# A pre-norm block on one core: statistics of one tile moved to ScalarE, the keys' sum moved to VectorE, one tile transposed by DMA

## The chip, the cores and the metric

The kernel runs on one core of one Trainium2 chip. The core has five engines that work side by side, each through its own instructions in order: TensorE (PE; its weight loads are shown as PEld), VectorE (DVE), ScalarE (ACT), GpSimd (POOL) and SyncE (SP), which here issues all transfers. They wait for each other through semaphores. The metric is the device time of one execution, in microseconds. Before the change it was 172.0 us, the median of three runs (171.96 to 172.21).

## The reference

The input x has 2048 rows of 512 columns, in bfloat16. Two sub-blocks follow one another, each with a layer norm in front and a residual around it:

```python
h  = x + attn(layernorm(x), wqkv, wo)      # 32 heads of 16 columns, linear attention
h2 = h + relu(layernorm(h) @ w1) @ w2      # 512 -> 1792 -> 512
```

The attention is linear: with phi(t) = (t + 1 if t > 0 else exp(t)) + 1e-6 it computes

```python
kv  = sum over rows of phi(k) (outer) v    # per head, 16 x 16
z   = sum over rows of phi(k)              # per head, 16
out = phi(q) @ kv / (phi(q) . z + 1e-6)
```

so no 2048 x 2048 matrix appears, but every key must be known before the first row of the attention's output is.

## The kernel before, in words

The 2048 rows are 16 tiles of 128 rows (an index t below), and four chunks of 512 rows, each of four tiles. Everything stays in the core's memory: x, the normalized rows, their transposes `lnT` (one per chunk), phi(k) of every tile (`pk`, kept in `pk_lo` and in the buffer that later holds the MLP's activations), phi(q) transposed (`pqT`), and all weights.

The stages, which overlap, are these.

- **First norm.** VectorE takes mean and variance of a tile (S, A: lines 237 and 238), ScalarE makes 1/sqrt of the variance from Ln and Exp (R: 243, 244), VectorE normalizes (N: 251).
- **Transposes.** Tiles 0 to 5 are transposed on TensorE (T: 270) and copied out by ScalarE (E: 280) or VectorE (V: 283); tiles 6 to 15 are transposed by DMA from SP (X: 291).
- **Keys.** Four matmuls per tile (K: 299), then phi: Exp and Relu on ScalarE (F, U: 317, 320), minimum and sum on VectorE (M, D: 324, 327).
- **G and z.** Values are never formed: G accumulates normalized-x-transposed times phi(k) over the 16 tiles in four PSUM banks (351), and kv follows from G and the value weights (381). The sum z is made on TensorE: for each of four column blocks, 16 matmuls, one per tile, with a right-hand side of ones and one output column (359).
- **Queries.** Per chunk, four groups of four matmuls (Q: 307) and the same phi (qF, qU, qM, qD).
- **Attention output.** kv is masked to heads (kx: 389) and multiplied by wo (m, copied out by mD: 399). The denominator of a chunk is a matmul of phi(q) with the masked z (d4: 406), its reciprocal Ln and Exp on ScalarE (dl4, dx4: 412, 417). In chunk 0 it is spread to all rows of a head by matmuls (rp: 422) and multiplied in on VectorE (rm: 428); in chunks 1 to 3 it is written to DRAM (wb: 434), read back broadcast in eight transfers (rb: 437, tile `rr`) and multiplied in (dm: 444). Four matmuls per tile then give the attention's output (h: 453), and VectorE adds x (hD: 459).
- **Second norm and MLP.** Statistics and mean removal on VectorE (s, a, n: 239, 240, 258), transposes by TensorE for chunk 0 (t, copied out by e: 286 or v: 289) and by DMA for the others (x: 292). The first product has 14 feature groups per chunk (p, and ph in halves for the first four of chunk 0: 468, 477), with ReLU on ScalarE or VectorE (pA: 483, pD: 488). The second has 14 matmuls per tile (f: 497). VectorE scales and adds (fo: 505), and SP writes the tile out (fd: 512).

The text called "block 1" in the change's short name is the norm and MLP part; its first chunk is the one that TensorE transposed.

The order is written out by hand as one list of words, `ORDER`. `T.3.3` means tile 3 through bank 3; `p.0.6.0` means chunk 0, feature group 6, bank 0; `lx.4.2` loads two tiles of x from tile 4 on. Each engine executes its own words in the order of the list, so a word that waits holds back all later words of its engine. Words of different engines do not hold each other except through data and buffers. SP's queue is one such list too, and the semaphores of its transfers are eight, used in turn: a transfer also waits for the one eight before it to land.

Of the kernel before, what the change touches and what calls it, by code (L numbers as in the profile page):

```python
# [58 lines left out]
def kernel(  # L59
# [27 lines left out]
    NO = 4  # L87

    const = ctx.enter_context(tc.tile_pool(name="const", bufs=1))
    big = ctx.enter_context(tc.tile_pool(name="big", bufs=1))  # L90
# [14 lines left out]
    wqkv_v = A_wqkv.rearrange("(k p) n -> p k n", p=P)  # L105
# [27 lines left out]
    z_sb = big.tile([P, KD], F32, name="z_sb")  # L133
    acts = [big.tile([P, KF, CW], BF16, name=f"at{i}") for i in range(2)]
    pk_lo = big.tile([P, 2, D], BF16, name="pk_lo")
    st = big.tile([P, NT, nc.vector.BN_STATS_DIM], F32, name="st")
# [7 lines left out]
    ld = big.tile([P, 2, CW], F32, name="ld")  # L144
    rd = big.tile([P, 2, CW], BF16, name="rd")
# [8 lines left out]
    def pk(t, n=1):  # L154
        return pk_lo[:, t : t + n, :] if t < 2 else acts[0][:, t - 2 : t - 2 + n, :]
# [38 lines left out]
    def op_mask():  # L194
# [4 lines left out]
    def op_maskh():  # L199
# [9 lines left out]
    def op_masks():  # L209
        op_mask()  # L210
        op_maskh()


    def op_gate():
        nc.gpsimd.memset(wk_sb[:, 0:4:2, 0:1], 0.0)

# [4 lines left out]
    def load_d(dst, src, k, n, queue=None):  # L221
        (queue or nc.sync).dma_start(out=dst[:, k : k + n, :], in_=src[:, k : k + n, :])

    op_lk = lambda k, n: load_d(wk_sb, wqkv_v[:, :, D : 2 * D], k, n)
    op_lkA = lambda k, n: load_d(wk_sb, wqkv_v[:, :, D : 2 * D], k, n, nc.scalar)
# [11 lines left out]
    op_S = lambda t: nc.vector.bn_stats(out=st[:, t, :], in_=x_nat[:, t, :])  # L237
    op_A = lambda t: nc.vector.bn_aggr(out=mv[:, t, :], in_=st[:, t, :])
# [116 lines left out]

    def op_z(jb, b):
        at_bank["z"] = b
        for t in range(NT):
            nc.tensor.matmul(  # L359
                bk[:, b, jb : jb + 1], lhsT=pk(t)[:, 0, jb * P : (jb + 1) * P], rhs=ones[:],  # L360
                start=(t == 0), stop=(t == NT - 1),
            )
# [40 lines left out]
    def op_d4(c, b):  # L403
        at_bank["d4", c] = b
        for jb in range(KD):
            nc.tensor.matmul(  # L406
                bk[jb * Q4 : (jb + 1) * Q4, b, :], lhsT=zhd[:, jb, :], rhs=pqT[c][:, jb, :],
                start=True, stop=True,
            )

    def op_dl4(c):
        nc.scalar.activation(
            out=ld[:, c % 2, :], in_=bk[:, at_bank["d4", c], :], func=ACT.Ln, bias=eps6[:], scale=1.0
        )

    def op_dx4(c):
        nc.scalar.activation(out=rd[:, c % 2, :], in_=ld[:, c % 2, :], func=ACT.Exp, scale=-1.0)

    def op_rp(c, jb, b):
        at_bank["rp", c, jb] = b  # L420
        rows = slice(jb * Q4, (jb + 1) * Q4)
        nc.tensor.matmul(
            bk[:, b, :], lhsT=erep[rows, :], rhs=rd[rows, c % 2, :], start=True, stop=True
        )
# [8 lines left out]
    def op_wb(c):  # L433
        nc.sync.dma_start(out=scr[c].rearrange("j h o n -> (j h) (o n)"), in_=rd[:, c % 2, :])
# [113 lines left out]
```

## Time and profile before

| | |
|---|---|
| median of three runs | 172.0 us |
| the profiled execution | 172.15 us |
| its span in the profile | 170.4 us |
| TensorE busy | 165.1 us (97%) |
| VectorE busy | 94.5 us (55%) |
| ScalarE busy | 66.3 us (39%) |
| transfers moved | 14.97 MB |

The span is shorter than the execution by 1.75 us, which lies around it. TensorE's busy time is modelled and matmuls overlap, so its share alone does not say how near it is to its limit; the chain that ended last does, since it goes back from the last instruction, step by step, to what released it. The groups of instructions give a line's total, the mean of one, and how long its engine sat idle just ahead of it.

### The profile page before, as it was taken

Reading aid. Unit: us, or ns where it says so; the run is one execution under the profiler, and the core shown is the slowest. Engines: PE = TensorE matmul, PEld = TensorE weight load, DVE = VectorE, ACT = ScalarE, POOL = GpSimd, SP = SyncE. Lnnn points to the kernel's source line nnn. Section 1 sums busy time; section 2 is a strip of 40 time slices with the busy share of each in tenths; the row PEclk is TensorE's granted clock in tenths of the full one; section 3 lists DMA queues with packets and bytes.
Section 4 is the critical chain, followed back from the end, with each engine's and each line's share of the span. In section 5 each row is a group of like instructions: output and inputs, shape, how many; then the busy total and the mean of one; then the engine's idle time right before and its main releaser. Section 6 shows DMA issues by size and latency. Waiting matters only on the chain.

```text
span 170.4 us, 2460 instructions
## 1 busy us (share of the span) xinstructions
PE 165.1 (97%) x949; PEld 81.4 (48%) x966; DVE 94.5 (55%) x199; ACT 66.3 (39%) x98; POOL 4.7 (3%) x21
## 2 busy tenths in 40 slices
PE   7999999999999999999999999999999999999993
PEld 7554344456444584444444444444444444444463
DVE  3999983215889945399050579105349613450252
ACT  3699754846796853403307213302133000310300
POOL 7300000000000000000000000000000000000000
PEclk9999999999999999999999999999999999999999
DMA  4963955999000022001433000544000240030004
GB/s 128 312 241 71 187 110 127 304 386 295 4 6 0 0 89 69 0 0 22 105 99 82 4 2 13 108 135 150 31 31 0 54 100 0 0 127 0 0 0 123
DMA packets 22619, 14.97 MB, mean 88 GB/s; under 512 B 13264, under 2 KB 21584, under 8 KB 22608
## 3 DMA queue, kind: packets, MB, share of 16 engines
q1 hardware_dynamic: 22608, 14.82, 31.1%
q8 instruction: 7, 0.11, 0.3%
q14 instruction: 4, 0.03, 0.1%
HBM read 9.44 MB, written 2.49 MB: 70 GB/s over the span
## 4 chain that ended last, share of the span: by engine, by line
PE 87%; ACT 4%; DMA 3%; DVE 2%; SPq 2%; issue 1%
PE bk L497 28%; PE bk L468 26%; PE bk L307 8%; PE bk L453 8%; PE bk L299 5%; PE bk L351 5%; DMA wk_sb<-in_A_wqkv_dram 3%; PE bk L477 2%; ACT eb L317 2%; ACT rb L320 1%; SPq L219 1%; PE bk L359 1%; PE bk L406 1%; PE bk L393 1%; PE bk L270 1%
## 5 line engine op out<-in xcount | busy, mean ns | idle before, releaser
L497 PE MATMUL bk<-w_sb,at 128*128 128x512 bf16 (+2 forms) x247 | 49.8, 355 | 0.3
L468 PE MATMUL bk<-lnT,w_sb 128*128 128x512 bf16 x204 | 46.8, 379 | 0.2
L483 ACT ACTIVATE at<-bk 128x1024 bf16<-128x1024 f32 x19 | 19.2, 1023 | 65.7 <-PE bk L468 62.9
L497 PEld LDWEIGHTS <-at 128*128 128x128 bf16 x252 | 23.4, 98 | 25.2 <-issue 0.5
L468 PEld LDWEIGHTS <-w_sb 128*128 128x128 bf16 x208 | 20.4, 98 | 24.3
L488 DVE TENSOR_SCALAR at<-bk 128x1024 bf16<-128x1024 f32 x9 | 11.0, 1225 | 24.7 <-PE bk L468 23.3
L505 DVE SCALAR_TENSOR_TENSOR gT<-bk,rstd,h_nat 128x512 bf16<-128x512 f32 (+2 forms) x18 | 12.2, 689 | 20.0 <-PE bk L497 16.3
L320 ACT ACTIVATE rb<-bk 128x1024 bf16<-128x1024 f32 (+1 forms) x18 | 16.7, 927 | 7.1 <-PE bk L307 5.6
L317 ACT ACTIVATE eb<-bk 128x1024 bf16<-128x1024 f32 (+1 forms) x18 | 16.6, 928 | 4.2 <-PE bk L299 3.5
L299 PE MATMUL bk<-wk_sb,lnT 128*128 128x512 bf16 x63 | 15.2, 379 | 0.6 <-ACT rb L320 0.3
L307 PE MATMUL bk<-lnT,wq_sb 128*128 128x512 bf16 x62 | 15.2, 379 | 0.1
L453 PE MATMUL bk<-m_sb,pqs 128*128 128x512 bf16 x63 | 15.1, 379 | 0.0
L459 DVE TENSOR_TENSOR h_nat<-bk,x_nat 128x512 bf16<-128x512 f32 x16 | 10.8, 687 | 6.8 <-PE bk L453 6.6
L351 PE MATMUL bk<-at,h_nat 128*128 128x512 bf16 x54 | 13.4, 379 | 0.1
L237 DVE BATCH_NORM_STATS2 st<-x_nat 128x6 f32<-128x512 bf16 x16 | 10.3, 677 | 1.8 <-DMA x_nat<-in_A_x_dram 1.8
L239 DVE BATCH_NORM_STATS2 st<-h_nat 128x6 f32<-128x512 bf16 x16 | 10.7, 682 | 0.1
L324 DVE TENSOR_SCALAR eb<-eb 128x1024 bf16<-128x1024 bf16 (+1 forms) x18 | 7.0, 389 | 5.9 <-ACT eb L317 5.9
L299 PEld LDWEIGHTS <-lnT 128*128 128x128 bf16 x64 | 6.1, 98 | 8.2 <-DMA lnT<-h_nat 0.8
L453 PEld LDWEIGHTS <-pqs 128*128 128x128 bf16 x64 | 6.3, 98 | 7.5
L351 PEld LDWEIGHTS <-h_nat 128*128 128x128 bf16 x64 | 6.1, 98 | 6.8
L307 PEld LDWEIGHTS <-wq_sb 128*128 128x128 bf16 x64 | 5.9, 98 | 6.4 <-issue 0.2
L444 DVE TENSOR_TENSOR pqs<-pqT,rr 128x1024 bf16<-128x1024 bf16 x6 | 4.0, 688 | 5.5 <-DMA rr<-scr 5.2
(61 smaller groups left out, 94.4 us busy)
## 6 DMA issues: line engine op xcount, KB each, us to landing
w_sb<-in_B_w_dram SPq DMA_DIRECT2D x4, 896.0 KB, 8.6
out_dram<-gT SPq DMA_DIRECT2D x15, 128.0 KB, 2.0
rr<-scr SPq DMA_DIRECT2D x24, 64.0 KB, 2.6
x_nat<-in_A_x_dram SPq DMA_DIRECT2D x2, 512.0 KB, 6.4
x_nat<-in_A_x_dram SPq DMA_DIRECT2D x4, 128.0 KB, 2.2
wk_sb<-in_A_wqkv_dram SPq DMA_DIRECT2D x2, 256.0 KB, 3.7
x_nat<-in_A_x_dram SPq DMA_DIRECT2D x2, 256.0 KB, 4.1
wq_sb<-in_A_wqkv_dram SPq DMA_DIRECT2D x2, 256.0 KB, 6.1
```

Source lines behind the costliest of these rows:

```text
L299: nc.tensor.matmul(bk[:, b, :], lhsT=lnT[c][:, kd, j * P : (j + 1) * P], rhs=wk_sb[:, kd, :], start=(kd == 0), stop=(kd == KD - 1),)
L307: nc.tensor.matmul(bk[:, b, :], lhsT=wq_sb[:, kd, j * P : (j + 1) * P], rhs=lnT[c][:, kd, :], start=(kd == 0), stop=(kd == KD - 1),)
L317: nc.scalar.activation(out=buf(eb, kind, i, n), in_=bank(at_bank[kind, i], n), func=ACT.Exp)
L320: nc.scalar.activation(out=buf(rb, kind, i, n), in_=bank(at_bank[kind, i], n), func=ACT.Relu)
L351: nc.tensor.matmul(bk[:, KD + kd, :], lhsT=ln_nat[:, t, kd * P : (kd + 1) * P], rhs=pk(t)[:, 0, :], start=(t == 0), stop=(t == NT - 1),)
L453: nc.tensor.matmul(bk[:, b, :], lhsT=pqs[:, (c * KD + jb) % NQ, j * P : (j + 1) * P], rhs=m_sb[:, jb, :], start=(jb == 0), stop=(jb == KD ...
L459: nc.vector.tensor_tensor(out=h_nat[:, t : t + n, :], in0=bank(at_bank["h", t], n), in1=x_nat[:, t : t + n, :], op=ALU.add,)
L468: nc.tensor.matmul(bk[:, b, :], lhsT=w1_sb[:, kd, f * P : (f + 1) * P], rhs=lnT[c][:, kd, :], start=(kd == 0), stop=(kd == KD - 1),)
L483: nc.scalar.activation(out=acts[c % 2][:, f : f + n, :], in_=bank(at_bank["p", c, f], n), func=ACT.Relu)
L488: nc.vector.tensor_scalar(out=acts[c % 2][:, f : f + n, :], in0=bank(at_bank["p", c, f], n), scalar1=0.0, scalar2=None, op0=ALU.max,)
L497: nc.tensor.matmul(bk[:, b, 0 : w * P], lhsT=acts[c % 2][:, f, j * P : (j + 1) * P], rhs=w2_sb[:, f, k * P : (k + w) * P], start=(f == 0), ...
L505: nc.vector.scalar_tensor_tensor(out=o_t[:, t % NO, cols], in0=bk[:, at_bank["f", t, k], 0 : w * P], scalar=rstd2[:, t : t + 1], in1=h_nat ...
```

## The change

Three things are changed in the code, and with them the whole order.

- **Tile 1's statistics** come from ScalarE: a copy that adds up the row (Sa), the negated mean (Sm), a square of the difference that adds up (Sq), and Ln and Exp (Sr). VectorE normalizes from them (Sn, in place of N.1).
- **z.** VectorE adds phi(k) of tiles 2 to 13, two tiles at a time, into fp32 (za, five additions of 1024 columns), adds the two halves (zf), and splits the sum into a bfloat16 part and a bfloat16 rest (zhi, zlo). z on TensorE then has six matmuls per column block instead of 16: the two parts and tiles 0, 1, 14 and 15.
- **Tile 0 of the second norm** is transposed by DMA (x.0) instead of on TensorE (t.0, e.0).

The denominators of all four chunks get buffers of their own (`ld`, `rd`), and those of chunks 2 and 3 are made together (`d4.2.0.2`).

In the new order, among much else: all four warm-up words of 512 columns stand ahead of the transposes; T.2 stands behind K.0; tile 3's copy is V instead of E; x tiles 4 and 5 are loaded ahead of wk; X.8 and X.9 stand ahead of all loads of wq and wv; keys of tiles 12 and 13 come before those of 10 and 11; gD stands behind zc; mD.0 and mD.2 have qM.1.2 between them; the first half of w2 (`l2.0.7`) is loaded behind wb.1 instead of among the other weights; wb.2 stands ahead of the transposes x.4 to x.7.

```diff
 ORDER = """
...
+table const masks warm.70.7.64 lx.0.1 S.0 A.0 warm.3.7 warm.1.7 lx.1.1 lx.2.1 S.2 Sa.1 lx.3.1 lx.4.2 lk.0.2
+lk.2.2 R.0.1 Sm.1 N.0.0.2 S.3 A.2 N.0.2.2 A.3 S.5 Sq.1 Sr.1 Sn.1 T.0.0.0.2 T.0.3.2.2 T.1.1 R.2.2 E.0.2.2
+E.0.0.2 E.1 N.3 T.3.3 S.4 A.5 A.4 R.4.2 lx.6.2 K.0.0 F.0.1 U.0.1 N.2 V.3 N.4 T.2.2 V.2 M.0.1 N.5 D.0.1 K.1.1
...
+A.13 M.4.2 S.12 D.4.2 A.12 R.12.2 X.7 X.6 G.3 K.7.3 K.6.2 X.8 X.9 F.6.2 U.6.2 S.11 S.10 A.10 N.12 M.6.2 A.11
+N.13 R.10.2 G.4 K.8.0 K.9.1 F.8.2 U.8.2 lq.0.2 X.12 X.13 D.6.2 N.11 S.14 S.15 M.8.2 A.14 N.10 A.15 D.8.2
+R.14.2 N.15 za.4 N.14 X.11 X.10 lv.0.2 lq.2.2 X.15 X.14 lv.2.2 l2.7.7 lo.0.2 lo.2.2 l1.2.2 l1.0.2 G.5 G.6 G.7
+K.12.0 K.13.1 G.8 K.11.3 K.10.2 F.12.2 U.12.2 F.10.2 U.10.2 G.9 Q.0.0.0 Q.0.1.1 za.6 za.8 M.10.2 D.10.2 za.10
+M.12.2 D.12.2 K.14.2 K.15.3 G.10 qU.0.0.2 F.14.2 qF.0.0.2 U.14.2 G.11 G.12 G.13 Q.0.2.0 Q.0.3.1 za.12 M.14.2
+qM.0.0.2 zf zhi D.14.2 G.14 zlo z.0.2 G.15 z.2.2 qF.0.2.2 qD.0.0.2 z.1.2 z.3.2 gA.2.2 qM.0.2.2 zc Q.1.1.3
+Q.1.0.2 gD.0.2 qU.0.2.2 qF.1.0.2 qU.1.0.2 zh qD.0.2.2 kv.0.4 kv.3.4 kv.2.4 kv.1.4 qM.1.0.2 kx qD.1.0.2 Q.1.2.0
+Q.1.3.1 qF.1.2.2 m.1.5 m.0.4 m.3.7 d4.0.3 m.2.6 mD.0.2 qM.1.2.2 mD.2.2 Q.2.0.2 dl4.0 dx4.0 qU.1.2.2 Q.2.1.3
+rp.0.0.4 rp.0.1.5 rp.0.2.6 rp.0.3.7 Q.2.3.1 Q.2.2.0 rm.0.0.2 rm.0.2.2 h.0.4 qD.1.2.2 hD.0 h.1.5 h.2.6 qU.2.0.2
+qU.2.2.2 qF.2.2.2 h.3.7 d4.1.4 qF.2.0.2 dl4.1 dx4.1 Q.3.2.0 Q.3.3.1 qF.3.2.2 qU.3.2.2 s.0 hD.1 hD.2 a.0 s.1
+n.0 a.1 hD.3 n.1 s.2 s.3 a.2 Q.3.0.2 t.1.5 Q.3.1.3 a.3 n.2 n.3 v.1 t.2.6 t.3.7 v.2 v.3 x.0 ph.0.2.0.0
...
+pA.0.0.2 p.0.6.0 p.0.7.1 p.0.5.3 p.0.4.2 wb.1 l2.0.7 rb.1.0 rb.1.6 rb.1.2 rb.1.4 rb.1.7 rb.1.5 rb.1.3 rb.1.1
...
+    zacc = big.tile([P, 2, D], F32, name="zacc")
+    zhl = big.tile([P, 2, D], BF16, name="zhl")
...
+    def op_Sa(t):
+        nc.scalar.activation(out=junk[:], in_=x_nat[:, t, :], func=ACT.Copy, accum_out=sums[:, 0:1])
+
+    def op_Sm(t):
+        nc.scalar.activation(out=sums[:, 1:2], in_=sums[:, 0:1], func=ACT.Copy, scale=-1.0 / D)
+
+    def op_Sq(t):
+        nc.scalar.activation(
+            out=junk[:], in_=x_nat[:, t, :], func=ACT.Square, bias=sums[:, 1:2], scale=1.0,
+            accum_out=sums[:, 2:3],
+        )
+
+    def op_Sr(t):
+        nc.scalar.activation(out=sums[:, 3:4], in_=sums[:, 2:3], func=ACT.Ln, bias=eps5[:], scale=1.0 / D)
+        nc.scalar.activation(out=sums[:, 3:4], in_=sums[:, 3:4], func=ACT.Exp, scale=-0.5)
...
+    def op_za(t):
+        nc.vector.tensor_tensor(out=zacc[:], in0=pk(2, 2) if t == 4 else zacc[:], in1=pk(t, 2), op=ALU.add)
+
+    def op_zf():
+        nc.vector.tensor_tensor(out=zacc[:, 0, :], in0=zacc[:, 0, :], in1=zacc[:, 1, :], op=ALU.add)
+
+    def op_zhi():
+        nc.vector.tensor_copy(out=zhl[:, 0, :], in_=zacc[:, 0, :])
+
+    def op_zlo():
+        nc.vector.tensor_tensor(out=zhl[:, 1, :], in0=zacc[:, 0, :], in1=zhl[:, 0, :], op=ALU.subtract)
+
     def op_z(jb, b):
         at_bank["z"] = b
-        for t in range(NT):
-            nc.tensor.matmul(
-                bk[:, b, jb : jb + 1], lhsT=pk(t)[:, 0, jb * P : (jb + 1) * P], rhs=ones[:],
-                start=(t == 0), stop=(t == NT - 1),
+        parts = [zhl[:, i, :] for i in range(2)] + [pk(t)[:, 0, :] for t in range(NT) if not 2 <= t < ZT + 2]
+        for i, part in enumerate(parts):
+            nc.tensor.matmul(
+                bk[:, b, jb : jb + 1], lhsT=part[:, jb * P : (jb + 1) * P], rhs=ones[:],
+                start=(i == 0), stop=(i == len(parts) - 1),
             )
```

More of the change, by code (lines that the diff above doesn't have):

```diff
@@ L207, in op_maskh, with load_d @@
             keep(rows, rows, [[-1, P]], DH - 1, DH)
[L209 to L215, printed above, removed]
     def op_lx(t, n):
         nc.sync.dma_start(out=x_nat[:, t : t + n, :], in_=rows_of(xf, t, n))
-    def load_d(dst, src, k, n, queue=None):
-        (queue or nc.sync).dma_start(out=dst[:, k : k + n, :], in_=src[:, k : k + n, :])
+    def load_d(dst, src, k, n):
+        nc.sync.dma_start(out=dst[:, k : k + n, :], in_=src[:, k : k + n, :])
     op_lk = lambda k, n: load_d(wk_sb, wqkv_v[:, :, D : 2 * D], k, n)
-    op_lkA = lambda k, n: load_d(wk_sb, wqkv_v[:, :, D : 2 * D], k, n, nc.scalar)
     op_lq = lambda k, n: load_d(wq_sb, wqkv_v[:, :, 0:D], k, n)
@@ L237, with op_Sn @@
     op_S = lambda t: nc.vector.bn_stats(out=st[:, t, :], in_=x_nat[:, t, :])
+    def op_Sa(t):
[10 more added lines that the diff above has]
+        nc.scalar.activation(out=sums[:, 3:4], in_=sums[:, 3:4], func=ACT.Exp, scale=-0.5)
+    def op_Sn(t, k=0, n=KD):
+        cols = slice(k * P, (k + n) * P)
+        nc.vector.tensor_scalar(
+            out=ln_nat[:, t, cols], in0=x_nat[:, t, cols], scalar1=sums[:, 1:2], scalar2=sums[:, 3:4],
+            op0=ALU.add, op1=ALU.mult,
+        )
     op_A = lambda t: nc.vector.bn_aggr(out=mv[:, t, :], in_=st[:, t, :])
@@ L399, in op_mD, with op_d4 @@
         nc.vector.tensor_copy(out=m_sb[:, jb : jb + n, :], in_=bank(at_bank["m", jb], n))
-    def op_d4(c, b):
-        at_bank["d4", c] = b
-        for jb in range(KD):
-            nc.tensor.matmul(
-                bk[jb * Q4 : (jb + 1) * Q4, b, :], lhsT=zhd[:, jb, :], rhs=pqT[c][:, jb, :],
-                start=True, stop=True,
-            )
+    def op_d4(c0, b0, n=1):
+        for c, b in zip(range(c0, c0 + n), range(b0, b0 + n)):
+            at_bank["d4", c] = b
+            for jb in range(KD):
+                nc.tensor.matmul(
+                    bk[jb * Q4 : (jb + 1) * Q4, b, :], lhsT=zhd[:, jb, :], rhs=pqT[c][:, jb, :],
+                    start=True, stop=True,
+                )
     def op_dl4(c):
         nc.scalar.activation(
-            out=ld[:, c % 2, :], in_=bk[:, at_bank["d4", c], :], func=ACT.Ln, bias=eps6[:], scale=1.0
+            out=ld[:, c, :], in_=bk[:, at_bank["d4", c], :], func=ACT.Ln, bias=eps6[:], scale=1.0
         )
     def op_dx4(c):
-        nc.scalar.activation(out=rd[:, c % 2, :], in_=ld[:, c % 2, :], func=ACT.Exp, scale=-1.0)
+        nc.scalar.activation(out=rd[:, c, :], in_=ld[:, c, :], func=ACT.Exp, scale=-1.0)
     def op_rp(c, jb, b):
@@ L422, in op_rp @@
         nc.tensor.matmul(
-            bk[:, b, :], lhsT=erep[rows, :], rhs=rd[rows, c % 2, :], start=True, stop=True
+            bk[:, b, :], lhsT=erep[rows, :], rhs=rd[rows, c, :], start=True, stop=True
         )
@@ L433, in op_wb @@
     def op_wb(c):
-        nc.sync.dma_start(out=scr[c].rearrange("j h o n -> (j h) (o n)"), in_=rd[:, c % 2, :])
+        nc.sync.dma_start(out=scr[c].rearrange("j h o n -> (j h) (o n)"), in_=rd[:, c, :])
     def op_rb(c, h):
```

67 lines of the change are left out of this document (27 added, 40 removed).

## The prediction

> **What bounds the kernel now.** I read the page first: how busy each engine is and whose work the final chain is.
>
> ```profile
> PE 165.1 (97%) x949; PEld 81.4 (48%) x966; DVE 94.5 (55%) x199; ACT 66.3 (39%) x98; POOL 4.7 (3%) x21
> ...
> PE 87%; ACT 4%; DMA 3%; DVE 2%; SPq 2%; issue 1%
> ```
>
> TensorE holds 87% of the chain. Its busy figure alone proves little, because matmuls overlap, so I take what one matmul costs from the chain in order of time (start, length, what). Between the edges quoted here it runs through TensorE with no other engine in it.
>
> ```profile
> 3.65 4.60 DMA wk_sb<-in_A_wqkv_dram
> ...
> 8.28 2.33 PE bk L299 x10
> ...
> 36.52 0.38 PE bk L359 x16
> ...
> 48.18 0.33 PE bk L422 x4
> 48.51 2.72 PE bk L307 x12
> 51.23 1.73 PE bk L453 x8
> ...
> 56.41 0.22 PE bk L270 x4
> ...
> 59.52 3.59 PE bk L477 x32
> ...
> 167.68 0.35 DVE gT L505
> ```
>
> A 512-wide matmul costs 1.73/8 = 0.216 us, a transpose 0.22/4 = 0.055, a one-column z matmul (L359) 0.38/16 = 0.024. So every removed TensorE instruction is worth its own time, and every wait inserted from 8.3 us on costs its own length. Stages from the query stage on show how little there is left to win (window, its length, busy of PE, PEld, DVE, ACT, POOL, then clock, DMA share, GB/s):
>
> ```profile
> 43.14:59.45 16.31, 16.20 (x103) 7.60 (x104) 14.85 (x29) 13.04 (x16) 0.00 (x0) 1.00 0.01 2
> 59.45:103.00 43.55, 43.34 (x218) 21.16 (x220) 23.35 (x42) 13.94 (x18) 0.00 (x0) 1.00 0.17 46
> 103.00:167.70 64.70, 64.33 (x324) 30.53 (x327) 27.65 (x50) 11.09 (x15) 0.00 (x0) 1.00 0.20 55
> ```
>
> TensorE idles 0.1, 0.2 and 0.4 us in these stages at full clock; VectorE is full in the first and half free in the MLP. Counting 0.216 per matmul (208 of the first MLP product, 48 of the h product, 210 of the second) gives the same.
>
> **The change, part by part.** Durations (busy, mean ns in the group; then idle before it) that the parts below use:
>
> ```profile
> L459 DVE TENSOR_TENSOR h_nat<-bk,x_nat 128x512 bf16<-128x512 f32 x16 | 10.8, 687 | 6.8 <-PE bk L453 6.6
> ...
> L327 DVE TENSOR_TENSOR pqT<-rb,eb 128x1024 bf16<-128x1024 bf16 x8 | 5.2, 680 | 0.0
> L258 DVE TENSOR_SCALAR hn<-h_nat,mv 128x512 bf16<-128x512 bf16 x16 | 5.0, 342 | 0.1
> ...
> L243 ACT ACTIVATE rstd<-mv,eps 128x2 f32<-128x2 f32 (+2 forms) x13 | 3.8, 292 | 4.0 <-DVE mv L238 3.9
> ...
> L417 ACT ACTIVATE rd<-ld 128x512 bf16<-128x512 f32 x4 | 2.5, 630 | 0.1
> L399 DVE CAST m_sb<-bk 128x1024 bf16<-128x1024 f32 x2 | 2.4, 1220 | 0.4 <-PE bk L393 0.4
> ```
>
> *Keys' sum.* z shrinks from 4x16 to 4x6 matmuls: 40 x 0.024 = **-0.96 us** on the path. [...]
>
> In exchange VectorE gets five fp32 additions of 1024 columns and three operations of 512. No fp32 addition out of SBUF is in the trace. Ends: 680 ns (1024 bf16 columns) and 1220 ns (1024 fp32 columns out of PSUM); I take 1220, since fp32 operands are what the two share: 5 x 1.22 + 3 x 0.61 = 7.9 us. [...]
>
> ```profile
> 33.64 1.29 DVE L327 TENSOR_TENSOR at<-rb,eb 128x1024 bf16<-128x1024 bf16 x2
> 40.38 1.23 DVE L376 CAST gT<-bk 128x1024 bf16<-128x1024 f32 x1 [5.45 <-PE bk L307]
> ```
>
> What hides them is VectorE's idle time in the G and z stage, 5.45 us in this one piece. What can still bind is the end of the series. In the new order the first query exp ends near 35.1 us by my walk; then zf, zhi, D.14, zlo at 0.61 to 0.68 each end D.14 near 37.3 and zlo near 37.9. TensorE reaches G.14 at 38.2 and z.0 at 39.1: spare 0.9 and 1.1. Cost 0; without the cover each late us costs one us.
>
> *Statistics of tile 1 on ScalarE.* VectorE loses S.1 and A.1. ScalarE gains Sa and Sq (128x512, 0.63 each by L417), Sm and the two parts of Sr (0.2 to 0.3 each): about 2 us, into the time before 6 us, where ScalarE idled for VectorE (3.9 us in the L243 row, most of it there). The first loads of x, 128 and 256 KB, landed after this long:
>
> ```profile
> x_nat<-in_A_x_dram SPq DMA_DIRECT2D x4, 128.0 KB, 2.2
> ```
> ```profile
> x_nat<-in_A_x_dram SPq DMA_DIRECT2D x1, 256.0 KB, 3.4
> ```
>
> R.0 now stands behind Sa: x tile 1, second on the queue (issued at 1.26), lands near 3.45 and Sa ends near 4.1, so the first normalized half is ready near 4.9. Warm-up matmuls, all now ahead of the transposes, run to 6.25 anyway. Behind S.5, which waits for x tiles 4 and 5 (issued 0.5 earlier than before, at 2.66, and landing by 6.1), VectorE does tile 1 near 6.6 and tile 3 near 7; K.0 is ready near 7.6 and still waits for wk at 8.25, since the same bytes stand ahead of it on SP's queue. Cost 0, with 0.6 spare. But T.2 moves behind K.0, out of that wait: +0.22. The copy of tile 3 goes from ScalarE to VectorE; both are ahead of K.3 by my walk, so 0.
>
> *Key stage.* The weight loads and matmuls of K.8 waited here:
>
> ```profile
> 18.66 1.89 PE L351 MATMUL bk<-at,h_nat 128*128 128x512 bf16 x8
> 20.81 1.90 PE L299 MATMUL bk<-wk_sb,lnT 128*128 128x512 bf16 x8 [0.26 <-ACT rb L320]
> ```
> ```profile
> 20.80 1.41 PEld L299 LDWEIGHTS <-lnT 128*128 128x128 bf16 x8 [0.75 <-DMA lnT<-h_nat]
> ```
> ```profile
> wq_sb<-in_A_wqkv_dram SPq DMA_DIRECT2D x1, 256.0 KB, 4.3
> lnT<-h_nat SPq DMA_TRANSPOSE x1, 4.2
> ```
>
> The eight matmuls from 18.66 are through at 20.39, so 0.42 is lost; X.8 took 4.2 us to land beside the wv and wq loads. The new SP order puts X.8 and X.9 ahead of lq and lv; at the 2.5 us of the median transpose (quoted below) they land near 18.4 and 19.6 for K.8 at 19.8: **-0.42**. The loads move: lv.0 and lq.2 now stand behind X.10, which waits for N.10 near 23.9. lq.2 is issued at about 25.7 and, at the 4.3 us of its like beside wv and two transposes, lands at 30.0; Q.0.0 needs it at 29.7: **+0.3** (between 0 and 0.4). X.14 (up to 4.2) lands with K.14's turn: 0.
>
> *Queries of chunk 0, block 1.* This chain of VectorE is tight:
>
> ```profile
> 45.62 2.36 DVE L399 CAST m_sb<-bk 128x1024 bf16<-128x1024 f32 x2 [0.36 <-PE bk L393]
> 48.41 0.43 DVE L324 TENSOR_SCALAR eb<-eb 128x1024 bf16<-128x1024 bf16 x1 [0.43 <-ACT eb L317]
> 48.75 2.35 DVE L428 TENSOR_TENSOR pqs<-bk,pqT 128x1024 bf16<-128x1024 f32 x2
> ```
>
> Before, rp started at 48.18, just as the second m copy ended (47.98), and h at 51.23 as rm ended (51.10). After, qM.1.2 (0.34) stands between the two copies, and two Q groups instead of three between rp and h. From the first m matmul, VectorE needs 0.64 + 4x1.135 + 0.34 + 0.1 = 5.6 us to the second rm; TensorE reaches h.0's third matmul after m 0.65, d4 0.33, m 0.22, four Q groups 3.45, rp 0.33, two matmuls 0.43 = 5.4. **+0.25**, against 0.2 lost there before: +0.05.
>
> *DMA transpose of tile 0.* x.0 takes t.0 off TensorE: **-0.22**, and its copy off ScalarE. It is issued when n.0 is through, and takes this long to land (SP's transposes of this kind and of the first kind):
>
> ```profile
> lnT<-hn SPq DMA_TRANSPOSE x12, 2.4
> lnT<-h_nat SPq DMA_TRANSPOSE x10, 2.5
> ```
>
> n.0 ends near 54.7 on VectorE; x.0 lands near 57.2, and the first MLP matmul comes near 58.0: 0.8 spare. From h (51.23) to the MLP (59.52) the chain took 8.3 us and its work 8.1 (32 matmuls 6.9, one d4 group 0.33, 16 transposes 0.88); with t.1 between the Q groups I find no wait, so a further **-0.2**.
>
> *Queue of SP behind it.* l2.0.7 (896 KB of w2) moves from 30 us to behind wb.1, ahead of the eight rr loads; the last of these shares l2's semaphore, so it waits for l2 to land. Loads of that size:
>
> ```profile
> w_sb<-in_B_w_dram SPq DMA_DIRECT2D x2, 896.0 KB, 6.1
> ```
> ```profile
> w_sb<-in_B_w_dram SPq DMA_DIRECT2D x1, 896.0 KB, 12.1
> ```
> ```profile
> rr<-scr SPq DMA_DIRECT2D x24, 64.0 KB, 2.6
> ```
>
> Issued near 56.5, alone, I take 6.1: landed 62.6, last rr at 65.2. dm.1.2, qM, qD and dm.1.0 (2.3 us) then end at 67.5, and h.4 is due at 69.4. Cost 0.
>
> *MLP.* The same work in another order. Walking banks and tiles I find everything in time, by 0.15 to 0.4 us at its tightest (fo.6 before h.14, the ReLU of features 4 and 5 before feature 9, the ReLU of 12 and 13 of chunk 1). Before lost about 0.3 net; I give the same.
>
> *Sum*: -0.96 + 0.22 - 0.42 + 0.3 + 0.05 - 0.22 - 0.2 = -1.2 us. The profiled execution took 172.15 (span 170.4 and 1.75 around it), 0.15 above the median of 172.0; so 170.95 for it and **170.8 us** for the median.
>
> **The rivals.**
>
> *All tight places hold*: lq.2 lands in time, no rm wait, and the MLP's 0.3 goes: 170.8 - 0.3 - 0.25 - 0.3 = 169.95. For it: VectorE is half idle. Against: each of these needs a spare that I could not find.
>
> *VectorE takes the gain back.* z ends the wait of zc and, behind it, of gD, which kv needs. After z, TensorE has two Q groups, 1.73 us; zc and gD need 0.2 + 0.1 + 1.23 = 1.5: 0.2 spare. In the old order gD stood ahead of z. If latencies add 0.5 here, 0.4 more at rm and 0.3 at one of the MLP's tight places, the time is 172.0. For it: three waits with the same engine; against: 14.9 of 16.3 us VectorE was already busy in the stage from 43 us on and still kept up.
>
> *w2 late, slower.* If l2.0.7 takes the 12.1 us of the last load, issued behind others, it lands at 68.6, the last rr at 71.2, dm.1.0 ends at 73.5 and h.4 waits 4.1: 174.9. It begins to cost at 8.0 us of landing and turns the forecast into a loss above 9.2. For it: the rr packets share the same engines. Against: nothing else large is in flight.
>
> **How the numbers follow.** Forecast 52% (own range 170.2 to 171.6), all tight places hold 14%, VectorE takes it back 20% (171.5 to 172.6), slower by w2 or by another transfer that lands late 14%. Taking 0.2%, 0.34 us, as what a measurement can tell: faster 0.52 + 0.14 + 0.07, same 0.06, slower 0.07 + 0.14. The range 169.8 to 172.8 leaves out most of the last case.
>
> **What would show it.** L392 with 24 matmuls in 0.6 us of the chain; no wait of the K loads on a DMA near 20 us; fp32 additions of about 1.2 us, D.14 before TensorE's turn; a wait of some 0.3 us on wq near 30 and of 0.25 on VectorE before rp or h; the MLP beginning near 58.1 instead of 59.5 and ending near 166.4. Wrong if K.0 starts late, if kv or h waits over 0.5 us, or if rr holds h.4.

## The result and the profile after

The changed kernel took 170.88 us, the median of four runs (170.47 to 170.94), against 172.11 (171.96 to 172.24) for the kernel before on the same chip: a ratio of 0.9924 with a 95% interval of 0.9906 to 0.9943. The profiled execution took 170.94 us at a span of 169.2, against 172.15 and 170.4. The page's busy times and the shares of the chain:

```profile
PE 163.5 (97%) x906; PEld 79.9 (47%) x922; DVE 105.1 (62%) x209; ACT 64.2 (38%) x98; POOL 4.8 (3%) x21
...
PE 94%; DMA 2%; issue 1%; SPq 1%; DVE 0%; DVEq 0%
```

TensorE has 43 matmul records fewer and now 94% of the chain instead of 87%; VectorE is 10.6 us busier, and the chain does not go through it for that. To place the difference I cut both spans where TensorE had done the same work: start of K.0, start of K.4, the point where ten key tiles and six G groups are done, start of kv, start of the MLP, and the end of the last matmul. The windows of after, in the columns of the prediction:

```profile
7.93:13.81 5.88, 5.83 (x39) 2.90 (x37) 5.88 (x20) 5.32 (x13) 0.00 (x0) 1.00 0.47 177
13.81:22.44 8.63, 8.63 (x40) 3.88 (x40) 8.44 (x25) 7.03 (x14) 0.00 (x0) 1.00 0.55 107
22.44:42.04 19.60, 19.44 (x111) 9.22 (x113) 16.57 (x30) 12.50 (x15) 0.00 (x0) 1.00 0.79 242
42.04:58.21 16.17, 16.12 (x100) 7.49 (x100) 14.65 (x28) 12.43 (x15) 0.00 (x0) 1.00 0.09 19
58.21:166.53 108.32, 107.78 (x541) 51.49 (x548) 54.36 (x93) 21.94 (x30) 0.00 (x0) 1.00 0.22 59
```

and of before (its stage from kv to the MLP, 16.31 us, stands in the prediction):

```profile
7.51:13.48 5.97, 5.73 (x35) 2.79 (x34) 5.89 (x18) 5.36 (x14) 0.00 (x0) 1.00 0.61 226
13.48:22.55 9.07, 8.81 (x41) 3.84 (x41) 8.81 (x27) 6.65 (x14) 0.00 (x0) 1.00 0.75 135
22.55:43.14 20.59, 20.43 (x150) 10.21 (x152) 8.73 (x20) 12.83 (x15) 0.00 (x0) 1.00 0.80 247
...
59.45:167.66 108.21, 107.67 (x540) 51.69 (x547) 50.98 (x90) 25.03 (x33) 0.00 (x0) 1.00 0.19 52
```

| stretch | before, us | after, us | difference | forecast |
|---|---|---|---|---|
| to the start of K.4 | 13.48 | 13.81 | +0.33 | +0.22 |
| ten key tiles and six G groups | 9.07 | 8.63 | -0.44 | -0.42 |
| from there to kv (holds z and lq.2) | 20.59 | 19.60 | -0.99 | -0.66 |
| kv to the MLP | 16.31 | 16.17 | -0.14 | -0.37 |
| MLP | 108.21 | 108.32 | +0.11 | 0 |
| sum | | | -1.13 | -1.23 |

Every stretch has the sign that was forecast or lies within 0.11 us of zero. The sum is right partly because three errors (+0.11, +0.23, +0.11) and one of -0.33 cancel. The reader is to look at VectorE in the third stretch: 16.57 us busy against 8.73, in a stretch that got 0.99 us shorter.

**z.** In the chain of after, a one-column group of six took 0.13 and the three other groups 0.43:

```profile
39.01 0.13 PE bk L392 x6
39.14 0.89 PE bk L369 x4
40.02 0.43 PE bk L392 x18
```

That is 0.56 us, where before had 0.38 (shown in the prediction) and these two:

```profile
38.65 0.38 PE bk L359 x16
...
40.78 0.78 PE bk L359 x32
```

1.54 - 0.56 = 0.98 us, at 0.43/18 = 0.024 per matmul as before.

**The head.** The path to the first key starts at a load now. From the chain, then from TensorE's timeline (start, length, what, and in brackets the idle time ahead of it with what ended it):

```profile
2.66 3.62 DMA x_nat<-in_A_x_dram
```
```profile
7.37 0.72 PE L288 MATMUL bk<-ident,h_nat 128*128 128x128 bf16 x8 [0.99 <-DVE h_nat L251]
7.93 1.03 PE L317 MATMUL bk<-wk_sb,lnT 128*128 128x512 bf16 x4
8.81 0.40 PE L288 MATMUL bk<-ident,h_nat 128*128 128x128 bf16 x4
9.05 1.89 PE L317 MATMUL bk<-wk_sb,lnT 128*128 128x512 bf16 x8
```

x tiles 4 and 5 landed at 6.28, S.5 could start only then, Sn.1 stood behind it, and T.1 waited for Sn.1. K.0 began at 7.93 and had wk. T.2 (8.81 to 9.05) then stands in the row of keys, 0.24.

**K.8.** No matmul waits; one weight load does, for X.9, inside the shadow of the matmul ahead of it (TensorE, then its weight loads):

```profile
19.85 1.89 PE L317 MATMUL bk<-wk_sb,lnT 128*128 128x512 bf16 x8
```
```profile
20.66 0.59 PEld L317 LDWEIGHTS <-lnT 128*128 128x128 bf16 x4 [0.28 <-DMA lnT<-h_nat]
```

**rp and rm.** Two waits stand here (TensorE, VectorE, weight loads):

```profile
47.78 0.64 PE L456 MATMUL bk<-rd,erep 32*128 32x512 bf16 x4
```
```profile
48.21 2.36 DVE L462 TENSOR_TENSOR pqs<-bk,pqT 128x1024 bf16<-128x1024 f32 x2 [0.23 <-PE bk L456]
```
```profile
50.62 2.70 PEld L487 LDWEIGHTS <-pqs 128*128 128x128 bf16 x14 [0.43 <-DVE pqs L462]
```

The four rp matmuls take from 47.78 to the next query group at 48.35, 0.57 instead of 0.33, because the last two of them go into the banks that mD.2 copies out until 47.98. VectorE is free at 47.98 but starts rm at 48.21, when rp's result is there. Then h.0's third matmul waits for the second rm: h's 16 matmuls take 50.09 to 53.75, 3.66, where 16 x 0.216 is 3.45. Together 0.24 + 0.21 = 0.45 us.

**MLP.** It begins at 58.21. One wait is inside it, at h.11 of chunk 2 (weight loads, then VectorE):

```profile
89.26 0.11 PEld L487 LDWEIGHTS <-pqs 128*128 128x128 bf16 x2 [0.47 <-DVE pqs L478]
89.86 0.11 PEld L487 LDWEIGHTS <-pqs 128*128 128x128 bf16 x2 [0.49 <-DVE pqs L478]
```
```profile
88.51 1.29 DVE L478 TENSOR_TENSOR pqs<-pqT,rr 128x1024 bf16<-128x1024 bf16 x2 [3.97 <-DMA rr<-scr]
```

VectorE idled 3.97 us for the last broadcast loads of chunk 2's denominators, which stand behind the transposes x.5 to x.4 and the write wb.3 on SP's queue. h.11's four matmuls took 89.26 to 90.31, 1.05 instead of 0.86, and began 0.14 late: 0.33 us.

### The profile page after: what moved, and what is told of

Its sections match the earlier page's. It is cut to its first block, busy times and chain, and to the rows that moved or that the text cites. A ratio compares the mean times of both kernels' runs of the same rounds, so it can differ in the third digit from the quotient of the medians.

```text
span 169.2 us, 2382 instructions
## 1 busy us (share of the span) xinstructions
PE 163.5 (97%) x906; PEld 79.9 (47%) x922; DVE 105.1 (62%) x209; ACT 64.2 (38%) x98; POOL 4.8 (3%) x21
## 3 DMA queue, kind: packets, MB, share of 16 engines
HBM read 9.44 MB, written 2.49 MB: 70 GB/s over the span
## 4 chain that ended last, share of the span: by engine, by line
PE 94%; DMA 2%; issue 1%; SPq 1%; DVE 0%; DVEq 0%
PE bk L531 28%; PE bk L502 26%; PE bk L487 9%; PE bk L325 8%; PE bk L317 8%; PE bk L369 8%; DMA x_nat<-in_A_x_dram 2%; PE bk L511 2%; PE bk L288 1%; SPq L214 1%; PE bk L440 1%; PE bk L426 1%; PE bk L414 1%; PE bk L456 0%; PE bk L392 0%
## 5 line engine op out<-in xcount | busy, mean ns | idle before, releaser
L517 ACT ACTIVATE at<-bk 128x1024 bf16<-128x1024 f32 x16 | 16.3, 1024 | 68.1 <-PE bk L502 63.0
L522 DVE TENSOR_SCALAR at<-bk 128x1024 bf16<-128x1024 f32 x12 | 14.7, 1222 | 16.3 <-PE bk L502 15.0
L493 DVE TENSOR_TENSOR h_nat<-bk,x_nat 128x512 bf16<-128x512 f32 x16 | 10.6, 681 | 7.1 <-PE bk L487 6.0
L261 ACT ACTIVATE rstd<-mv,eps 128x2 f32<-128x2 f32 (+2 forms) x12 | 3.5, 294 | 9.2 <-DVE mv L258 7.7
```

The lines of the kernel that those rows point to most:

```text
L493: nc.vector.tensor_tensor(out=h_nat[:, t : t + n, :], in0=bank(at_bank["h", t], n), in1=x_nat[:, t : t + n, :], op=ALU.add,)
L517: nc.scalar.activation(out=acts[c % 2][:, f : f + n, :], in_=bank(at_bank["p", c, f], n), func=ACT.Relu)
L522: nc.vector.tensor_scalar(out=acts[c % 2][:, f : f + n, :], in0=bank(at_bank["p", c, f], n), scalar1=0.0, scalar2=None, op0=ALU.max,)
```

## The experiments

All were measured beside the kernel before on their chip, in three groups. Its median was 172.00 beside E1 to E4, 172.10 beside E5 to E8 and 172.38 beside E9 to E12. The changed kernel itself ran again in the third group (E9). Runs of one kernel lie up to 2.0 us apart (the kernel before beside E5 to E8, 171.55 to 173.54; E2 1.5), which is why medians of 5 to 12 runs are told, and why differences of a few tenths are read from the traces too.

### E1 and E2: z back on TensorE, without and with the additions

E1 takes the eight words of the sum on VectorE out and lets TensorE sum all 16 tiles; E2 does only the second, so that VectorE makes the sums and nobody uses them. In the cut below the eight words, which stand at six places of the order, are put on one line.

```diff
-za.4 za.6 za.8 za.10 za.12 zf zhi zlo
-        parts = [zhl[:, i, :] for i in range(2)] + [pk(t)[:, 0, :] for t in range(NT) if not 2 <= t < ZT + 2]
+        parts = [pk(t)[:, 0, :] for t in range(NT)]
```

> The changed kernel with z as before: 4x16 one-column matmuls on TensorE, and VectorE's additions, their sum and its two halves taken out of the order. Theory (z stood on TensorE's path at 0.024 us a matmul): 40 x 0.024 = 0.96 us slower than the changed kernel's 170.9, so 171.9 (171.6 to 172.1). Rival (z was hidden, since kv waits for the copies of G anyway): 170.9 to 171.2.

> As the run before it, with VectorE's additions left in; their result is not used. Theory (the additions lie in VectorE's idle time): the same time as without them, within 0.2 us. Rival (the additions hold the minimum and sum of the last keys back, and so G): 0.3 us or more slower than without them.

Measured: E1 171.91 (ratio to before 0.9994, 0.9979 to 1.0009), E2 171.83 (0.9990, 0.9976 to 1.0004). Both are 1.0 us above the changed kernel's 170.88, and 1.1 and 1.0 above E4 below, which ran beside them. The chain of E1 has the old 64 matmuls:

```profile
39.37 0.38 PE bk L391 x16
...
40.63 1.18 PE bk L391 x48
```

1.56 us against 0.56. So the matmuls are worth their own time, and this one part is as large as four fifths of the net gain of 1.2 us. E2 with the additions is not slower than E1 without them. The windows from the start of K.4 to kv say it more closely (E1, then E2):

```profile
14.17:43.40 29.23, 29.23 (x194) 14.09 (x193) 17.77 (x46) 19.51 (x28) 0.00 (x0) 1.00 0.68 194
13.95:43.18 29.23, 29.23 (x193) 14.08 (x192) 25.06 (x54) 19.52 (x28) 0.00 (x0) 1.00 0.69 194
```

VectorE (the third busy time) does 7.3 us more in E2, and the stretch is as long; in the changed kernel it is 8.63 + 19.60 = 28.23, 1.00 shorter. That the additions are hidden is shown, not only argued.

### E3: tile 0 of the second norm back on TensorE

```diff
-x.0
-Q.3.0.2 t.1.5
+Q.3.0.2 t.0.4 e.0 t.1.5
```

> The changed kernel with tile 0 of the second norm transposed on TensorE (t.0) and copied out by ScalarE (e.0), as before, instead of by DMA. Theory: at least the four transposes' 0.22 us slower, 171.1; up to 0.5 slower, 171.4, if the copy, which ScalarE makes when it has the last query groups to do, delays the bank of a first MLP group. Rival (the DMA landed so late that it only replaced one wait by another): 170.9 or faster.

Measured: 171.14 (0.9960, 0.9946 to 0.9973), 0.26 above the changed kernel's median and 0.31 above E4's. Four transposes are 0.22. The size fits; runs of this kernel spread from 170.75 to 171.87, so the medians do not measure the 0.22 closely. In its trace the piece from h to the MLP is 8.40 us long (50.82 to 59.22), where the changed kernel's is 8.12: 0.28.

### E4: statistics of tile 1 back on VectorE

```diff
-lx.1.1 lx.2.1 S.2 Sa.1 lx.3.1
+lx.1.1 S.1 A.1 lx.2.1 S.2 lx.3.1
-R.0.1 Sm.1 N.0.0.2
+R.0.1 N.0.0.2
-S.5 Sq.1 Sr.1 Sn.1
+S.5 R.1.1 N.1
```

> The changed kernel with tile 1's statistics on VectorE again. Theory (VectorE waits for x tiles 4 and 5 anyway and K.0 is bound by wk): 0 to 0.2 us slower, 170.9 to 171.1. Rival (the 0.85 us that VectorE saves stand on the path to the first keys): 0.5 to 0.9 slower, 171.4 to 171.8.

Measured: 170.83 (0.9938, 0.9925 to 0.9950): no difference. This part of the change buys nothing in the median.

### E5: the old place of the wv and wq loads, ahead of X.8 and X.9

```diff
-K.6.2 X.8 X.9
+K.6.2 lv.0.2 lq.0.2 X.8 X.9
```

(with the two words taken from their later places)

> The changed kernel with lv.0 and lq.0 ahead of X.8 and X.9 on SP's queue, as the kernel before had them. Theory (loads beside a transpose stretch its landing from 2.5 to some 4 us): X.8 lands near 21.4, K.8 was due at 19.85, so TensorE waits 0.8 to 1.6 us there and the time is 171.7 to 172.5. Rival (a transpose lands after 2.5 us whatever runs beside it): X.8 near 19.7, at most 0.3 slower.

Measured: 172.54 (1.0012, 0.9989 to 1.0035), 1.7 us above the changed kernel's 170.88, 1.8 to 2.1 above E6 to E8, which ran beside it, and as slow as before. In its trace, TensorE and its weight loads:

```profile
21.02 1.90 PE L316 MATMUL bk<-wk_sb,lnT 128*128 128x512 bf16 x8 [1.13 <-ACT rb L337]
```
```profile
21.01 1.41 PEld L316 LDWEIGHTS <-lnT 128*128 128x128 bf16 x8 [1.62 <-DMA lnT<-h_nat]
```

The G group ahead ended at 19.72, so 1.3 us is lost: X.8 was issued at 17.32 and landed 3.7 us later. TensorE's line names ScalarE for its wait, the weight loads name the transfer; the second is right, since X.8 is what came last. The place of two loads on SP's queue is worth more than z here (1.7 us in the medians against 1.0). Before, with the loads in the same place, lost only 0.42: there X.8 was issued at 16.55 for a turn at 20.39, 3.8 us ahead, and in E5 at 17.32 for a turn at 19.72, 2.4 us ahead.

### E6: the first half of w2 back among the other weights

```diff
-wb.1 l2.0.7 rb.1.0
+wb.1 rb.1.0
-l2.7.7 lo.0.2
+l2.7.7 l2.0.7 lo.0.2
```

> The changed kernel with the first half of w2 loaded among the other weights, as before, instead of ahead of the rr loads. Theory (rr lands more than 1 us before h.4 needs its product either way): within 0.2 us of 170.9. Rival (the load of 896 KB delays rr and so h.4): 0.3 us or more faster.

Measured: 170.70 (0.9924, 0.9900 to 0.9948). It is 0.18 below the changed kernel's median, inside the spread, and its ratio is the same to four digits. The late load costs nothing that can be measured. Its neighbours did land later beside it: in the changed kernel's trace it landed in 5.5 us, and the broadcast loads behind it took up to 4.4 instead of the 2.6 of before (2.7 at most), which dm.1.2 on VectorE waited 0.64 us for, and TensorE not at all.

### E7: both copies of m ahead of qM.1.2

```diff
-mD.0.2 qM.1.2.2 mD.2.2
+mD.0.2 mD.2.2 qM.1.2.2
```

> The changed kernel with the query's minimum qM.1.2 behind the two copies of m on VectorE instead of between them. Theory (VectorE's series copy, copy, product, product sets when h may go on, and only two Q groups are there to cover it): the wait at rp goes, a wait of the same size stands at h, 0 to 0.2 us faster. Rival (the minimum's 0.34 us is what TensorE waited for): 0.4 us faster.

Measured: 170.61 (0.9912, 0.9891 to 0.9934). In its trace rp no longer waits, and h waits longer (TensorE, then VectorE):

```profile
47.61 0.40 PE L455 MATMUL bk<-rd,erep 32*128 32x512 bf16 x4
48.00 1.89 PE L324 MATMUL bk<-lnT,wq_sb 128*128 128x512 bf16 x8
49.72 3.93 PE L486 MATMUL bk<-m_sb,pqs 128*128 128x512 bf16 x16
```
```profile
48.05 2.35 DVE L461 TENSOR_TENSOR pqs<-bk,pqT 128x1024 bf16<-128x1024 f32 x2 [0.23 <-PE bk L455]
```

rp takes 0.39, h 3.86 (to 53.58) instead of 3.66. What rp gains h loses: 0.47 us is lost here against 0.45. From kv to the MLP the two kernels take the same, 16.18 and 16.17. So rp's bank is not what sets the loss, and the order of the copies isn't either: in E7 VectorE is free at 47.82 and begins rm at 48.05, when rp's result is there. In both kernels rm begins 0.43 to 0.44 us after rp's start, and the two rm then take 2.36 us, while TensorE has rp itself, two query groups and two matmuls of h (0.33 + 1.73 + 0.43 = 2.49 from rp's start) to fill 0.43 + 2.36 + 0.15 = 2.94; the 0.15 lie between the end of the second rm and the end of the weight load that waits for it. The difference is the 0.45. So what is lost is this path from rp over rm to h, with two query groups beside it where the kernel before had three. An order with a third group there was not run.

### E8: the broadcast loads of chunk 2 together

```diff
-rb.2.4 rb.2.6 x.5
+rb.2.4 rb.2.6 rb.2.5 rb.2.7 rb.2.1 x.5
-wb.3 rb.2.5 rb.2.7 rb.2.1
+wb.3
```

> The changed kernel with the last three rr loads of chunk 2 issued with the first five, ahead of x.4 to x.7 and of wb.3. Theory (h.11 waited 0.33 us for the product with rr, whose last loads stood behind four transposes and a write): the wait goes, 0.3 us faster, 170.6. Rival (the wait only moves to h.9 or to a first MLP group of chunk 1): within 0.1 us of the changed kernel.

Measured: 170.47 (0.9897, 0.9874 to 0.9920), the lowest median of all. The weight loads' group and TensorE's rows at h.11:

```profile
L486 PEld LDWEIGHTS <-pqs 128*128 128x128 bf16 x64 | 6.1, 98 | 7.9 <-DVE pqs L461 0.4 <-issue 0.4
```
```profile
89.47 1.03 PE L486 MATMUL bk<-m_sb,pqs 128*128 128x512 bf16 x4
90.34 1.03 PE L501 MATMUL bk<-lnT,w_sb 128*128 128x512 bf16 x4
```

The wait on L477 (dm) is gone, and h.11 takes 0.87. In all ten kernels that keep the changed kernel's place of these loads (after, E1 to E7, E9, E10), the group shows 0.6 to 1.0 us of weight-load idle time on dm; in E8, E11 and E12 it lists none. From the start of the MLP's first matmuls in the chain to fo of the last tile, E8 takes 107.85 us (58.73 to 166.58), and E11 and E12 also 107.85; the ten take 107.92 (E2, E5) to 108.18 (after), E9 108.00. So the loads' place costs 0.07 to 0.33 us, about 0.14 in the middle of the ten.

### E9 to E12: the changed kernel again, an earlier T.2, and sums of the edits

E10 was to remove the +0.22 of T.2 and the wait behind x tiles 4 and 5 in one: T.2 and T.1's normalization ahead of S.5 and S.4, and the later statistics behind the first keys.

```diff
-A.3 S.5 Sq.1
+A.3 Sq.1
-N.3 T.3.3 S.4 A.5 A.4 R.4.2 lx.6.2 K.0.0 F.0.1 U.0.1 N.2 V.3 N.4 T.2.2 V.2 M.0.1 N.5 D.0.1 K.1.1
+N.3 T.3.3 N.2 T.2.2 S.5 S.4 V.3 V.2 A.5 A.4 lx.6.2 K.0.0 F.0.1 U.0.1 R.4.2 M.0.1 D.0.1 N.5 N.4 K.1.1
```

E11 is E7 and E8 together, E12 is E7, E8 and E10.

> The changed kernel itself once more, to stand beside the three below on one chip: 170.9, within 0.2 us.

> The changed kernel with its head put another way: the statistics of tiles 5 and 4 behind the norm of tiles 1, 3 and 2, T.2 ahead of K.0 again, R.4 behind the first Exp and Relu. Theory (in the changed kernel the late x tiles 4 and 5 hold tile 1, and T.2 stands in TensorE's way at 0.22 us): the keys start with the landing of wk, 0.2 to 0.4 us faster, 170.5 to 170.7. Rival (ScalarE or X.9, 0.3 us behind, give it back before 21 us): within 0.1 us.

> The changed kernel with the two copies of m together and the eight rr loads of chunk 2 together. Theory (two separate waits of TensorE, each on its path): the gains of the two runs add up, 0.4 to 0.6 us faster than the changed kernel, 170.3 to 170.5. Rival (one slack serves both): not over 0.3 us.

> The changed kernel with the other head, the copies together and the rr loads together. Theory: 0.6 to 0.9 us faster than the changed kernel, 170.0 to 170.3; if the head gives nothing, as the run with the two others alone.

Measured: E9 170.89 (0.9910, 0.9885 to 0.9935), E10 171.59 (0.9951, 0.9928 to 0.9974), E11 170.56 (0.9891, 0.9868 to 0.9915), E12 171.33 (0.9935, 0.9912 to 0.9957).

E10 missed: 0.7 us slower than E9. In its trace the first keys do run in a row from 8.01 without T.2 among them, and the time is lost later:

```profile
13.45 0.81 PE L368 MATMUL bk<-pk_lo,h_nat 128*128 128x512 bf16 x3 [0.38 <-DVE pk_lo L344]
...
21.69 1.04 PE L316 MATMUL bk<-wk_sb,lnT 128*128 128x512 bf16 x4 [0.31 <-DMA lnT<-h_nat]
```

R.4, now behind F.0 and U.0 on ScalarE, and their own new place behind D.0 made N.5 and N.4 late on VectorE (10.61); D.1 stood behind them and behind two more statistics (12.98), so G.1 waited. The normalizations that follow were late too, X.7 was issued at 14.34 instead of 13.66, and K.9 waited for X.9 at 21.69. The first queries began at 30.34 instead of 29.35. The statistics of later tiles look idle in the head, but the row of DMA transposes depends on them: moved back, they cost three times what T.2 costs (0.7 us against 0.24). E12 is 0.77 above E11, the same loss.

E11 is 0.33 below E9, where 0.4 to 0.6 had been expected; E7's part has nothing to give (above), so what is shown is E8's gain. In the two profiles, whose keys began at 7.41 and 7.43, the MLP accounts for 0.15 of it. E8 and E11 beat both kernels in the median; against the changed kernel their intervals overlap. So a gain of 0.1 to 0.3 us is supported by the wait that is gone and by the length of the MLP; that it is as much as the medians' 0.3 to 0.4 is not shown.

**The head from one execution to the next.** E9 is the changed kernel, but its profiled execution began its keys half a microsecond earlier:

```profile
7.41 1.09 PE L317 MATMUL bk<-wk_sb,lnT 128*128 128x512 bf16 x4
```
```profile
58.08 3.49 PE bk L511 x32
...
166.08 0.35 DVE gT L539
```

The load of x tiles 4 and 5 had landed after 3.0 us instead of 3.6. In the ten profiles with the same head (after, E1 to E3, E5 to E9, E11) it landed after 2.9 to 4.4 us, and K.0 began at 7.38 to 8.66. Which load holds the keys differs. Where this one landed after 3.5 to 4.4 us (after, E1, E3, E6, E7), K.0 began about 1.65 us behind the landing and ran through. In E2, E5 and E8 the second half of K.0 waited for wk, which landed at 8.2 to 8.7, as the prediction had it (E5):

```profile
8.27 0.59 PE L316 MATMUL bk<-wk_sb,lnT 128*128 128x512 bf16 x2 [0.29 <-DMA wk_sb<-in_A_wqkv_dram]
```

In E9 and E11 the load landed after 3.0 us and held nobody. There the keys began earliest, and K.9 gave 0.2 of it back: it waited for X.9, which landed after 3.2 and 3.3 us (E9's weight loads; the eight matmuls of K.8 and K.9 took 2.07 instead of 1.89):

```profile
20.40 0.55 PEld L317 LDWEIGHTS <-lnT 128*128 128x128 bf16 x4 [0.50 <-DMA lnT<-h_nat]
```

The rest follows the head: E9's profiled execution took 170.46, after's 170.94, with ends at 166.08 and 166.56. E4 has the statistics of tile 1 in their old place; its load landed after 3.2 and K.0 began at 8.00, later than in E9, so the ScalarE statistics may pay where x lands early. Its median does not show it, and this stays open.

## Why the prediction was right, point by point

The time came within 0.1 us and inside the own range, and the likeliest case is what happened. That it came so close is partly luck: four steps were wrong and nearly cancelled, and the head alone moved the start of the keys by over 1 us between executions.

- **"It runs through TensorE with no other engine in it": not everywhere.** Between two of the edges quoted, from 10.64 to 20.81 us, the chain of before goes through ScalarE and VectorE:

```profile
10.64 0.60 ACT eb L317
...
19.88 0.93 ACT rb L320
```

  The price of a removed matmul comes from edges behind this piece, and in the piece TensorE's rows show only one wait, the 0.26 ahead of K.8; so no term of the sum fell with it.
- **z, -0.96: right.** Measured 0.98 in the chain and 1.0 by undoing it. The trace of after repeats the 0.024 us per one-column matmul (0.43/18; 0.38/16 before).
- **The additions hidden at 1.22 each, with D.14 near 37.3 and zlo near 37.9: right.** VectorE's rows after:

```profile
26.57 2.48 DVE L377 TENSOR_TENSOR zacc<-zacc,at 128x1024 f32<-128x1024 f32 x2
...
36.24 0.43 DVE L383 CAST zhl<-zacc 128x512 bf16<-128x512 f32 x1
...
37.19 0.68 DVE L386 TENSOR_TENSOR zhl<-zacc,zhl 128x512 bf16<-128x512 f32 x1
```

  The additions take 1.22 to 1.23 and zlo ends at 37.87. D.14 ended at 37.26 and G.14 began at 37.98, a spare of 0.7 instead of 0.9. The cheap end of 0.68 per addition is out. The 1.22 was the author's estimate, from casts of 1024 fp32 columns out of PSUM; the trace of after is the first that shows such an addition. zf, with 512 columns, took 0.69, where 0.61 to 0.68 had been assumed.
- **"Cost 0, with 0.6 spare" in the head: wrong.** The step took 6.1 for the landing of x tiles 4 and 5 and saw wk at 8.25 behind it as the limit. In the profiled execution wk landed at 7.7, earlier than that, and the load at 6.28, and T.1 waited 0.99 us for the normalization behind S.5. There K.0 began at 7.93, and 0.1 us is the whole loss against the forecast; but the spare was none, and in other executions the same load cost up to 0.7 more. The limit that the step had named, wk near 8.25, held in three of the ten profiles with this head (E2, E5, E8). S.5 ahead of Sn.1 on VectorE is the wait that the prediction had named and priced at zero.
- **T.2 behind K.0, +0.22: right** (0.24), although E10 showed that it can't be had back by moving the statistics.
- **K.8, -0.42: right** (-0.44 in the stretch). E5, with the two loads ahead of X.8 again, showed the wait again and larger: X.8 landed after 3.7 us, where after had 2.5, and 1.3 us was lost with the new order around it. The spare was smaller than forecast, though: X.9 was issued at 17.64 and landed after 3.0 us, at 20.64 instead of 19.6, when K.9 was due at 20.71; in E9, E11 and E12 it came about 0.2 too late.
- **"lq.2 is issued at about 25.7 and ... lands at 30.0; +0.3": wrong.** It was issued at 26.04 and landed 3.2 us later at 29.3, not after 4.3: the price was one landing of one like load, read once. Q.0.0 began at 29.35 and ran its eight matmuls without a gap:

```profile
29.35 1.89 PE L325 MATMUL bk<-lnT,wq_sb 128*128 128x512 bf16 x8
31.08 1.89 PE L317 MATMUL bk<-wk_sb,lnT 128*128 128x512 bf16 x8
```

  Its lower bound, 0, was the value.
- **The rm chain, +0.25 against 0.2: the place right, the path and the size wrong.** 0.45 was lost. The step set VectorE's series of copies, qM and rm against TensorE's work (5.6 and 5.4, which is 0.2 apart, not 0.25). But VectorE's series did not decide: rm begins 0.23 us after VectorE is free, since rp's result comes only then, and E7 lost 0.47 with the copies in another order. What decides is rp, then two rm, then h (2.94 us), beside only two query groups (2.49 with rp and two matmuls of h).
- **t.0 off TensorE, -0.22: right** by E3 (0.28 in the trace, 0.26 to 0.31 in the medians). x.0 was issued at 54.94 and landed after 2.4, and the MLP began at 58.21, forecast 58.0. **The further -0.2 from h to the MLP** was taken by h's own wait: 8.38 us before, 8.12 after, -0.26 with the 0.22 of t.0 in it.
- **w2 behind wb.1 at 0: right** (E6). The rival needed 8.0 us of landing; it took 5.5.
- **"MLP: everything in time": wrong.** h.11 was not among the tight places I had listed. In the new order h.11 stands behind three of chunk 1's feature groups, where it stood behind ten before, and the last three of its eight broadcast loads still stand behind four transposes on SP's queue, as all eight did before, and now behind wb.3 too. That cost 0.33 us in the profiled execution; over the ten profiles compared with E8 it is 0.07 to 0.33. It stayed near zero net because before, as the prediction put it, lost about 0.3 too (108.21 against 108.32).
- **Rivals.** VectorE takes the gain back: of its three waits kv's did not come (gD ended at 41.78, kv began at 42.04 right behind the queries), rm's came at 0.45, 0.2 over the forecast where the rival needed 0.4, and one in the MLP came, through a load. All tight places hold: lq.2 alone did. Statistics of tile 1: no effect in the median (E4).

## What to carry to other kernels

TensorE holds 94% of the chain here, and the matmuls removed from it were worth about their own time (0.96 us forecast for z, 0.98 and 1.0 measured). The additions, given to VectorE where it had a visible idle piece, were free until a named consumer (29.23 us from K.4 to kv with and without them, E2 and E1). Both came out to a tenth of a microsecond from the rows of before. What could not was every step that hangs on a transfer: a landing time read once is a sample (2.9 to 4.4 us for one load here), so give a step that waits for a load a spare of the load's spread, and walk every word that is moved along the transfer queue to its consumer, also far behind the edit; for every consumer that is moved up, look at when its transfers land. An order that moves work back from an idle-looking head must be followed to the transfers that this work feeds.

## What the runs showed of the hardware that was not expected

- Each of tile 1's two accumulating ScalarE operations had a second instruction behind it that reads the accumulator, 0.19 us each, at 3.92 and 5.28 (ScalarE's timeline of after, which begins with the first of them); the prediction's sum of about 2 us for ScalarE left it out:

```profile
3.38 0.63 ACT L234 ACTIVATE junk<-x_nat 128x512 bf16<-128x512 bf16 x1 [1.30 <-DMA x_nat<-in_A_x_dram]
3.92 0.19 ACT L234 ACTIVATION_READ_ACCUMULATOR junk<-x_nat 128x1 f32 x1
```

- A cast of 512 fp32 columns to bfloat16 out of SBUF on VectorE took 0.43 us, cheaper than the 0.61 that had been assumed from the casts out of PSUM; the fp32 additions had no such discount (0.69 for 512 columns, 1.22 for 1024).
- The same 256 KB load, with the same queue ahead of it, landed after 2.9 to 4.4 us in different executions, and where it came last the whole kernel moved with it. A DMA transpose (X.8) landed after 2.5 us ahead of the loads and after 3.7 behind two of 256 KB (E5), and TensorE paid 1.3 us for these 1.2 us and an issue 1.0 us later (17.32 instead of 16.35).
